# The order of the first weight rows and input tiles on two DMA queues, in a fused two-layer kernel

## The chip, the cores and the metric

One core of one Trainium2 chip. The metric is the device time of one execution in microseconds (us). Before the change it was 1615.32 us, the median of three executions (1615.10 to 1616.07).

## The reference

Two rounds of attention and feed-forward over 2048 tokens of width 1024, all in bf16. Attention is local and dilated: 32 heads, 8 keys each, 2 apart. Only the first step matters here: the normalization of the first 512 tokens and their product with the query weights.

```python
x = A_x                                              # (1, 2048, 1024)
x = x + _A_ref(_layernorm(x, axis=-1), A_wqkv, A_wo) # qkv = x @ wqkv, first of all
x = x + _B_ref(_layernorm(x, axis=-1), B_w1, B_w3, B_w2)
x = x + _A_ref(_layernorm(x, axis=-1), A_wqkv, A_wo)
x = x + _B_ref(_layernorm(x, axis=-1), B_w1, B_w3, B_w2)
```

## The kernel before

The kernel lists operations with what they read and write, a list scheduler in Python puts them in order, and they are emitted in that order. Each engine runs its own list in order. The keys in `reads` and `writes` only order the list: a wait on the chip exists only where the framework sees that two instructions touch the same tile. Two DMA queues are used: SyncE's ("SP") and ScalarE's ("AQ").

At the start, the query weights come in as eight rows, row k being 128 input dimensions by 1024 outputs (256 KB). The 512 tokens come as tiles 0 to 3 (256 KB each, tile 0 in two halves). Tiles 0 and 1 are only centred (their average is subtracted), transposed by TensorE, and multiplied with the rows as these arrive. Tiles 2 and 3 are normalized on VectorE first, and their product with all eight rows (64 matmuls at L524) follows.

```python
for hh in range(2):
    dma(128, x_sb[0][:, hh * 512:(hh + 1) * 512], ..., 0, queue="AQ" if hh else "SP")
dma(256, x_sb[1][:], xin[:, 1, :], [], ..., 0, queue="AQ")
rows = q_weights(0, "k", load=False)
wslots[0] = rows[:2]
for kk in (0, 1, 3, 4):
    rows[2](kk)                       # 256 KB each, on SyncE's queue
rows[2](2, queue="AQ")
load_x(0, 3, 4)                       # tile 3, SyncE
rows[2](5)
rows[2](6, 2)                         # rows 6 and 7 in one DMA of 512 KB
...
act(0.75, ...)                                               # ScalarE: half of tile 0's sum
dma(256, x_sb[2][:], xin[:, 2, :], [("part", 1)], ..., 0, queue="AQ")   # tile 2
act(1.15, ... accum_out=mean[:, 1:2]), [...], [("xn", 3), ("mean", 1)], -9)   # tile 1's average
...
wslots[1] = q_weights(1, "s")         # K weights: two DMAs of 1 MB on SyncE, issued after the rows
...
for t0, t1_ in ((0, 2), (2, 4), (4, 5), (5, 6), (6, 7), (7, 8)):
    dma(256 * (t1_ - t0), wo[:, t0:t1_, :], ...)
```

TensorE's order is fixed: transposes of tile 0 (L428), rows 0 and 1 on tile 0 (L510), transposes of tile 1, row 2 on tile 0, rows 0 to 2 on tile 1, rows 3 to 6 on both, transposes of tiles 2 and 3, row 7, then L524, then the K product (L347).

One thing isn't in the kernel's text but in the built program: DMAs of both queues are given eight completion semaphores in turn. From the ninth DMA on, an issue first waits until the last user of its semaphore has landed.

Of the kernel before, what the change touches and what calls it, by code (L numbers as in the profile page):

```python
# [156 lines left out]
def kernel(  # L157
# [15 lines left out]
    KT = D // P  # L173
# [26 lines left out]
    def alloc(name, shape, dt=BF16):  # L200
        return sb.tile(shape, dt, name=name)
# [13 lines left out]
    wo = alloc("wo", [P, KT, D])  # L215
# [18 lines left out]
    mean = alloc("mean", [P, 2], FP32)  # L234
    rsx = alloc("rsx", [P, NB], FP32)
    oT = [alloc(f"oT{i}", [P, KT, TCH]) for i in range(2)]
# [8 lines left out]
    def t1(n):  # L245
        return 0.15 + n / 960.0

    def dve(dur, emit, reads, writes, cls=2, **kw):
        return pr.add("DVE", dur, emit, reads, writes, cls, **kw)
# [4 lines left out]
    def dma(kb, dst, src, reads, writes, cls=3, transpose=False, queue="SP"):  # L254
        def emit(op):
            if queue == "AQ":
                nc.scalar.dma_start(dst, src)
            elif transpose:
                nc.sync.dma_start_transpose(dst, src)
            else:  # L260
                nc.sync.dma_start(dst, src)  # L261
        return pr.add(queue, 0.45, emit, reads, writes, cls, size=kb * 1024)
# [34 lines left out]
    def load_x(c, j0=0, j1=TPC, after=()):  # L297
        for j in range(j0, j1):
            n = c * TPC + j
            dma(256, x_sb[n][:], xin[:, n, :], after, [("x", n, 0), ("x", n, 1)], 0 if c == 0 else 3)  # L300
# [41 lines left out]
    def mm8(a, pairs, first, last, reads, lane=0, ncol=512, takes=True):  # L342
        n = len(pairs)

        def emit(op):
            for i, (w, r) in enumerate(pairs):
                nc.tensor.matmul(bank[a.bank][:, 0:ncol], lhsT=w, rhs=r, start=first and i == 0,  # L347
                                 stop=last and i == n - 1)
        return pr.add("PE", n * (ncol / 2400.0 + 0.0025), emit, reads, [], takes=[a], lane=lane, lag=0.17)

    def evac(add, dur, emit, last_mm, reads, writes, a, cls=0, **kw):
        op = add(dur, emit, reads, writes, cls, gives=[a], **kw)
        op.deps.add(last_mm)
        return op
# [3 lines left out]
    def q_weights(which, split, load=True, after=()):  # L358
        ids = [take_slot(), take_slot()]
        if not load:  # L360
            def row(kk, n=1, after=(), **kw):
                i = ids[kk // 4]
                v = slot[i][:].rearrange("p (k c) -> p k c", k=4)
                dma(256 * n, v[:, kk % 4:kk % 4 + n, :], wqkv_v[:, kk:kk + n, which * D:(which + 1) * D], after,
                    [("w", i, kk % 4 + z) for z in range(n)], 0, **kw)
            return ids, split, row
        for h, i in enumerate(ids):
            if split != "c":
                v = slot[i][:].rearrange("p (k c) -> p k c", k=4)
                dma(1024, v, wqkv_v[:, 4 * h:4 * h + 4, which * D:(which + 1) * D], after,  # L370
                    [("w", i, k) for k in range(4)], 3)
            else:
                v = slot[i][:].rearrange("p (k c) -> p k c", k=KT)
                dma(1024, v, wqkv_v[:, :, which * D + h * 512:which * D + (h + 1) * 512], [],
                    [("w", i, k) for k in range(4)], 3)
        return ids, split
# [18 lines left out]
    def q_tile(l, c, which, ws, b, keep=None):  # L395
        for m0 in range(0, KT, 2):
            i = n_sgt[0] % 4
            n_sgt[0] += 1
            for m in (m0, m0 + 1):
                a = Acc()  # L400
                lk = [q_lhs(ws, kk, m) for kk in range(KT)]
                op = mm8(a, [(w, xnT[b][:, kk, :]) for kk, (w, _) in enumerate(lk)], True, True,
                         list({k for _, k in lk}) + [("xnT", b, j) for j in range(TPC)] +
                         [("xnT", b, j, h) for j in range(TPC) for h in range(2)])
                evac(act, 0.59, lambda _, a=a, i=i, m=m: nc.scalar.copy(sgt[i][:, m % 2, :], bank[a.bank][:]), op, [],  # L405
                     [("sgt", i, m % 2)], a)
                if keep:
                    evac(act, 0.4, lambda _, a=a, m=m: nc.scalar.copy(keep[1][:, m, HALO:], bank[a.bank][:, 0:TCH]),
                         op, [], [(keep[0], m)], a)
            dma(256, spill_view(l, which, m0, c, ws[1] == "s"), sgt[i][:], [("sgt", i, 0), ("sgt", i, 1)],  # L410
                [("d", l, which, c, m0)], 1)
# [8 lines left out]
    def transposed(src, keys, dst, dkeys):  # L420
        for h, add, fn, dur in ((0, dve, nc.vector.tensor_copy, 0.42), (1, act, nc.scalar.copy, 0.59)):
            a = Acc()
            k0 = 4 * h

            def tr(op, a=a, k0=k0):
                pt = bank[a.bank][:].bitcast(BF16)
                for k in range(4):
                    nc.tensor.transpose(pt[:, k * P:(k + 1) * P], src[:, (k0 + k) * P:(k0 + k + 1) * P], ident[:])  # L428
            tro = pr.add("PE", 0.25, tr, [keys[h], "ident"], [], takes=[a], lag=0.17, lane=2)

            def emit(op, a=a, k0=k0, fn=fn):
                pt = bank[a.bank][:].bitcast(BF16)
                fn(dst[:, k0:k0 + 4, :], pt[:, 0:4 * P].rearrange("p (k t) -> p k t", k=4))
            evac(add, dur, emit, tro, [], dkeys[k0:k0 + 4], a, cls=-9)

    def q_first():
        for hh in range(2):
            dma(128, x_sb[0][:, hh * 512:(hh + 1) * 512], xin[:, 0, hh * 512:(hh + 1) * 512], [], [("x", 0, hh)], 0,
                queue="AQ" if hh else "SP")
        dma(256, x_sb[1][:], xin[:, 1, :], [], [("x", 1, 0), ("x", 1, 1)], 0, queue="AQ")  # L440
        rows = q_weights(0, "k", load=False)
        wslots[0] = rows[:2]
        for kk in (0, 1, 3, 4):
            rows[2](kk)
        rows[2](2, queue="AQ")
        load_x(0, 3, 4)
        rows[2](5)
        rows[2](6, 2)
        b, q, stats, root, apply = ln(0, first=True)
        ce = hT[:, 8:16, :]  # L450
        dve(0.45, lambda _: nc.vector.tensor_scalar(xn[2][:, 0:512], x_sb[0][:, 0:512], 0.0, 0.0, op0=ALU.add,
# [7 lines left out]
        act(1.15, lambda _: nc.scalar.activation(xn[3][:], x_sb[1][:], ACTF.Copy, scale=1.0 / D,  # L459
                                                 accum_out=mean[:, 1:2]), [("x", 1, 0), ("x", 1, 1)],  # L460
            [("xn", 3), ("mean", 1)], -9)
        for j in range(2):
            for h0, h1 in ((0, 1), (1, 2)) if j == 0 else ((0, 2),):
                dve(0.5 if j else 0.32, lambda _, j=j, c0=512 * h0, c1=512 * h1: nc.vector.tensor_scalar(
                    xn[j][:, c0:c1], x_sb[j][:, c0:c1], mean[:, j:j + 1], None, op0=ALU.subtract),
                    [("x", j, 0), ("x", j, 1), ("mean", j)], [("xn", j)] + [("xn", j, h) for h in range(h0, h1)], -9)
            transposed(xn[j], [("xn", j, h) for h in range(2)], ce[:, :, j * P:(j + 1) * P],
                       [("ce", j, k) for k in range(KT)])
# [72 lines left out]
        for which, key, tile_ in ((1, "kT", kT), (2, "vT", vT)):  # L541
            dve(0.11, lambda _, tile_=tile_: nc.vector.memset(tile_[:, :, 0:HALO], 0.0), [], [(key, "h")], 1)
            q_tile(0, 0, which, wslots[which], b, (key, tile_))
        for t0, t1_ in ((0, 2), (2, 4), (4, 5), (5, 6), (6, 7), (7, 8)):
            dma(256 * (t1_ - t0), wo[:, t0:t1_, :], wo_v[:, t0:t1_, :], [("d", 0, 2, 0, 6)], [("wo", t0)], 3)
        stage_no[0] += 1

# [24 lines left out]
    def t_stage(l, half):  # L572
# [46 lines left out]
        oh = half % 2  # L619
# [7 lines left out]
        for j in range(TCH // P):  # L627
            n = tok0 // P + j
            for hh in range(2):
                a = Acc()  # L630
                op = mm8(a, [(oT[oh][:, t, j * P:(j + 1) * P], wo[:, t, hh * 512:(hh + 1) * 512]) for t in range(KT)],
                         True, True, [("oT", oh, t) for t in range(KT)] + [("wo", t) for t in (0, 2, 4, 5, 6, 7)], lane=1)
                xs = x_sb[n][:, hh * 512:(hh + 1) * 512]
                evac(dve, t1(512), lambda _, xs=xs, a=a: nc.vector.tensor_tensor(xs, xs, bank[a.bank][:], op=ALU.add),  # L634
                     op, [("x", n, hh)], [("x", n, hh)], a)
# [72 lines left out]
    def attend(l, c):  # L708
        for r in range(R):
            t_stage(l, c * R + r)  # L710

    q_first()
    attend(0, 0)
    for c in range(1, NCH):
# [47 lines left out]
```

## Time and profile before

| | before |
|---|---|
| median of three executions | 1615.32 us |
| span of the profiled execution (which took 1616.3 us) | 1614.5 us |
| TensorE busy | 1609.9 us |
| TensorE's waits after the warm-up | 0.27 us for row 1, 0.79 us for rows 6-7 |

In the views, PE is TensorE and PEld its weight loads, DVE is VectorE, ACT is ScalarE; SPq and ACTq are the issue of a DMA on SyncE's and ScalarE's queue. `slot` is a weight buffer, `x` an input tile, `xn` a centred or normalized tile, `hT` and `xnT` transposed ones, `bank` an accumulator; L510 is a line of the kernel, and L285 the warm-up, ten matmuls on constants that use no loaded data. A line of three dots marks lines left out.

The first and third lines of the page, of the kernel before; busy time, share of the span and number of instructions of each engine:

```profile
span 1614.5 us, 19227 instructions
...
PE 1609.9 (100%) x7610; PEld 763.0 (47%) x7610; DVE 1121.6 (69%) x1904; ACT 330.8 (20%) x527; POOL 5.3 (0%) x28
```

TensorE's waits over the whole span, before (engine and line, what it waited for, us in total, times, the longest):

```profile
PE bank L510 <- DMA slot<-in_A_wqkv_dram: 1.1, 2, 0.8
PE bank L285 <- PEq L746: 0.8, 1, 0.8
```

The chain of waits in the first 24 us, before (start, us, what):

```profile
1.19 0.42 SPq L261
...
1.66 5.32 DMA slot<-in_A_wqkv_dram
6.98 0.02 issue
7.00 0.33 SPq L261
7.32 0.04 issue
7.37 5.98 DMA slot<-in_A_wqkv_dram
13.35 0.05 issue
13.40 1.05 PE bank L510 x8
...
16.21 6.99 PE bank L524 x64
```

This chain is the whole argument for the change: row 1 is loaded (to 6.98), its landing lets row 5 be issued (7.00), rows 6-7 are issued right behind it (7.37) and land at 13.35, and TensorE goes on at 13.40. TensorE's own timeline, before (start, us, engine, line, operation, tiles, form, count, idle time just before and what ended it):

```profile
5.02 1.00 PE L428 MATMUL bank<-ident,xn 128*128 128x128 bf16 x8
6.15 0.61 PE L510 MATMUL bank<-hT,slot 128*128 128x128 bf16 x8
7.03 0.62 PE L510 MATMUL bank<-hT,slot 128*128 128x128 bf16 x8 [0.27 <-DMA slot<-in_A_wqkv_dram]
7.57 0.62 PE L428 MATMUL bank<-ident,xn 128*128 128x128 bf16 x8
8.03 4.58 PE L510 MATMUL bank<-hT,slot 128*128 128x128 bf16 x56
13.40 1.05 PE L510 MATMUL bank<-hT,slot 128*128 128x256 bf16 x8 [0.79 <-DMA slot<-in_A_wqkv_dram]
14.28 1.06 PE L428 MATMUL bank<-ident,xn 128*128 128x128 bf16 x16
15.18 1.04 PE L510 MATMUL bank<-hT,slot 128*128 128x256 bf16 x8
16.05 7.15 PE L524 MATMUL bank<-xnT,slot 128*128 128x256 bf16 x64
```

From L524's start on TensorE never waits again. In every trace of this study the last weight load of the program comes 1595.6 to 1595.7 us after the first one of L524, except where the clock fell or the matmuls were ordered otherwise. So the start of L524 is the number to read: what it gains or loses, the span gains or loses.

ScalarE's list, before (ACTq is the issue of a DMA on its queue):

```profile
3.61 0.63 ACT L454 ACTIVATE xn<-x 128x512 bf16<-128x512 bf16 x1 [1.38 <-DMA x<-in_A_x_dram]
...
5.40 0.34 ACTq L257 DMA_DIRECT2D x<-in_A_x_dram  x1
5.85 1.06 ACT L459 ACTIVATE xn<-x 128x1024 bf16<-128x1024 bf16 x1 [1.52 <-DMA x<-in_A_x_dram]
```

The line at 5.40 is the issue of tile 2. It was meant to go out once the first average is on its way, but it waited until 5.38, when row 0 landed and its semaphore came free.

### The profile page before, as it was taken

Reading aid. Unit: us, or ns where it says so; the run is one execution under the profiler, and the core shown is the slowest. Engines: PE = TensorE matmul, PEld = TensorE weight load, DVE = VectorE, ACT = ScalarE, POOL = GpSimd, SP = SyncE. Lnnn points to the kernel's source line nnn. Section 1 sums busy time; section 2 is a strip of 40 time slices with the busy share of each in tenths; the row PEclk is TensorE's granted clock in tenths of the full one; section 3 lists DMA queues with packets and bytes.
Section 4 is the critical chain, followed back from the end, with each engine's and each line's share of the span. In section 5 each row is a group of like instructions: output and inputs, shape, how many; then the busy total and the mean of one; then the engine's idle time right before and its main releaser. Section 6 shows DMA issues by size and latency. Waiting matters only on the chain.

```text
span 1614.5 us, 19227 instructions
## 1 busy us (share of the span) xinstructions
PE 1609.9 (100%) x7610; PEld 763.0 (47%) x7610; DVE 1121.6 (69%) x1904; ACT 330.8 (20%) x527; POOL 5.3 (0%) x28
## 2 busy tenths in 40 slices
PE   9999999999999999999999999999999999999999
PEld 6555544444444444444444444444444444444444
DVE  5898888889889888888898729884298832211211
ACT  5423322021211222113211032110321101101110
POOL 1000000000000000000000000000000000000000
DMA  9834755395548664858545487355873564454451
GB/s 312 232 104 147 228 170 167 118 227 170 171 134 248 193 197 128 218 166 248 174 140 158 162 243 227 126 170 177 254 223 119 155 184 156 144 172 154 156 164 45
DMA packets 350777, 285.80 MB, mean 177 GB/s; under 512 B 72288, under 2 KB 344928, under 8 KB 350688
## 3 DMA queue, kind: packets, MB, share of 16 engines
q1 hardware_dynamic: 350112, 283.67, 58.4%
q8 instruction: 59, 0.97, 0.2%
q10 hardware_dynamic: 576, 0.92, 0.2%
q14 instruction: 30, 0.25, 0.0%
HBM read 238.94 MB, written 29.36 MB: 166 GB/s over the span
## 4 chain that ended last, share of the span: by engine, by line
PE 99%; DMA 1%; SPq 0%; issue 0%; DVE 0%
PE bank L347 98%; DMA slot<-in_A_wqkv_dram 1%; PE bank L524 0%; PE bank L510 0%; SPq L261 0%; PE bank L428 0%; DVE x L689 0%
## 5 line engine op out<-in xcount | busy, mean ns | idle before, releaser
L347 PE MATMUL bank<-xnT,slot 128*128 128x512 bf16 x5056 | 1094.2, 379 | 0.0
L347 PEld LDWEIGHTS <-slot 128*128 128x128 bf16 x5056 | 518.2, 102 | 572.9
L347 PE MATMUL bank<-slot,hT 128*128 128x512 bf16 (+2 forms) x1848 | 389.2, 373 | 0.0
L659 DVE TENSOR_TENSOR hT<-sg,bank 128x512 bf16<-128x512 bf16 x224 | 153.5, 685 | 212.5 <-PE bank L347 203.2
L265 DVE TENSOR_TENSOR scr<-scr 128x1024 bf16<-128x1024 bf16 (+3 forms) x576 | 292.8, 537 | 2.1
L347 PEld LDWEIGHTS <-hT 128*128 128x128 bf16 x1848 | 178.5, 98 | 208.7
L657 ACT ACTIVATE sg<-bank 128x512 bf16<-128x512 f32 x224 | 133.7, 597 | 654.1 <-PE bank L347 633.9
L265 DVE TENSOR_TENSOR scr<-qT,kT 128x2048 bf16<-128x2048 bf16 x128 | 153.9, 1218 | 73.1 <-DMA kT<-qkv_d 71.5
L405 ACT CAST sgt<-bank 128x512 bf16<-128x512 f32 x184 | 107.7, 586 | 288.9 <-PE bank L347 280.6
L265 DVE TENSOR_TENSOR scr<-pA,vT 128x2048 bf16<-128x2048 bf16 x128 | 152.7, 1219 | 0.4
L689 DVE TENSOR_TENSOR x<-x,bank 128x512 bf16<-128x512 bf16 (+1 forms) x66 | 43.7, 670 | 122.6 <-PE bank L347 122.4
L347 PE MATMUL bank<-wo,oT 128*128 128x512 bf16 x512 | 113.1, 379 | 0.0
L313 DVE BATCH_NORM_STATS2 st<-x 128x6 f32<-128x512 bf16 x124 | 81.5, 680 | 12.2 <-DMA x<-in_A_x_dram 11.8
L347 PEld LDWEIGHTS <-oT 128*128 128x128 bf16 x512 | 50.1, 98 | 60.4
L634 DVE TENSOR_TENSOR x<-x,bank 128x512 bf16<-128x512 bf16 x64 | 43.9, 685 | 35.6 <-PE bank L347 34.5
L320 ACT ACTIVATE sd<-mv,epst 128x4 f32<-128x4 f32 (+1 forms) x17 | 5.1, 298 | 183.7 <-DVE mv L316 183.4
L594 DVE STREAM_TRANSPOSE pB<-pA 128x2048 bf16<-128x2048 bf16 x16 | 37.0, 2310 | 0.4
L617 DVE STREAM_TRANSPOSE pA<-pB 128x2048 bf16<-128x2048 bf16 x16 | 37.0, 2310 | 0.4
L657 ACT ACT_TABLE_LOAD x20 | 25.7, 1283 | 51.0 <-PE bank L347 50.8
L265 DVE TENSOR_TENSOR pA<-scr 128x256 bf16<-128x256 bf16 x128 | 35.5, 284 | 0.3
L265 DVE TENSOR_TENSOR oT<-scr 128x256 bf16<-128x256 bf16 x128 | 33.8, 285 | 0.1
L327 DVE TENSOR_SCALAR xn<-x,mv,rstd 128x1024 bf16<-128x1024 bf16 x62 | 30.8, 541 | 3.7 <-DMA xnT<-xn 3.6
(60 smaller groups left out, 211.5 us busy)
## 6 DMA issues: line engine op xcount, KB each, us to landing
slot<-in_B_w_dram SPq DMA_DIRECT2D x160, 1024.0 KB, 6.0
slot<-in_A_wqkv_dram SPq DMA_DIRECT2D x28, 1024.0 KB, 5.2
qkv_d<-sgt SPq DMA_DIRECT2D x92, 256.0 KB, 3.6
qT<-qkv_d SPq DMA_DIRECT2D x16, 512.0 KB, 5.0
slot<-in_B_w_dram SPq DMA_DIRECT2D x16, 512.0 KB, 5.6
kT<-qkv_d SPq DMA_DIRECT2D x14, 544.0 KB, 6.7
vT<-qkv_d SPq DMA_DIRECT2D x14, 544.0 KB, 5.7
out_dram<-x SPq DMA_DIRECT2D x31, 128.0 KB, 4.4
```

What stands on the lines that cost most here:

```text
L265: return lambda _: nc.vector.tensor_tensor(o, a, b, op=op)
L313: dve(0.67, lambda _, hh=hh: nc.vector.bn_stats(st[q][:, j, hh, :], x_sb[n][:, hh * 512:(hh + 1) * 512]), [("x", n, hh)] + list(after), [( ...
L320: act(0.3, lambda _: nc.scalar.activation(sd[q][:, j0:j1], mv[q][:, j0:j1, 1], ACTF.Sqrt, bias=epst[:]), [("mv", q, j) for j in range(j0, ...
L327: dve(0.5, lambda _: nc.vector.tensor_scalar(xn[j][:], x_sb[n][:], mv[q][:, j, 0:1], rstd[q][:, j:j + 1], op0=ALU.subtract, op1=ALU.mult), ...
L347: nc.tensor.matmul(bank[a.bank][:, 0:ncol], lhsT=w, rhs=r, start=first and i == 0, stop=last and i == n - 1)
L405: evac(act, 0.59, lambda _, a=a, i=i, m=m: nc.scalar.copy(sgt[i][:, m % 2, :], bank[a.bank][:]), op, [], [("sgt", i, m % 2)], a)
L594: dve(2.31, lambda _: nc.vector.transpose(psmT[:].rearrange("p c d -> p (c d)"), psm[:].rearrange("p w s -> p (w s)")), allA, ["pB"])
L617: dve(2.31, lambda _: nc.vector.transpose(At[:].rearrange("p w s -> p (w s)"), AeT[:].rearrange("p c d -> p (c d)")), ["pB"], allA)
L634: evac(dve, t1(512), lambda _, xs=xs, a=a: nc.vector.tensor_tensor(xs, xs, bank[a.bank][:], op=ALU.add), op, [("x", n, hh)], [("x", n, hh) ...
L657: evac(act, 0.6, lambda _, i=i, a=ag: nc.scalar.activation(sg[i][:], bank[a.bank][:], ACTF.Silu), og, [], [("sg", i)], ag, table="silu")
L659: evac(dve, t1(512), lambda _, i=i, a=au, f=f: nc.vector.tensor_tensor(hT[:, f, :], sg[i][:], bank[a.bank][:], op=ALU.mult), ou, [("sg", i ...
L689: evac(dve, t1(cn), lambda _, xs=xs, a=a, cn=cn: nc.vector.tensor_tensor(xs, xs, bank[a.bank][:, 0:cn], op=ALU.add), op, [("x", n, hh)], [ ...
```

## The change

The intent: give rows 0 to 5 and 7 to SyncE's queue in the order in which TensorE wants them, let ScalarE's queue carry the tiles 1 and 2 and, early, row 6, and so have the last rows sooner. One load of wo is merged so that the number of DMAs stays the same.

```diff
-        for kk in (0, 1, 3, 4):
+        for kk in range(5):
             rows[2](kk)
-        rows[2](2, queue="AQ")
         load_x(0, 3, 4)
         rows[2](5)
-        rows[2](6, 2)
+        rows[2](7)
 ...
             [("xn", 3), ("mean", 1)], -9)
+        rows[2](6, queue="AQ", after=[("mean", 1)])
 ...
-        for t0, t1_ in ((0, 2), (2, 4), (4, 5), (5, 6), (6, 7), (7, 8)):
+        for t0, t1_ in ((0, 2), (2, 4), (4, 6), (6, 7), (7, 8)):
```

(The list of wo keys that the matmuls read is adapted likewise.)

More of the change, by code (lines that the diff above doesn't have):

```diff
@@ L631, in t_stage @@
                 op = mm8(a, [(oT[oh][:, t, j * P:(j + 1) * P], wo[:, t, hh * 512:(hh + 1) * 512]) for t in range(KT)],
-                         True, True, [("oT", oh, t) for t in range(KT)] + [("wo", t) for t in (0, 2, 4, 5, 6, 7)], lane=1)
+                         True, True, [("oT", oh, t) for t in range(KT)] + [("wo", t) for t in (0, 2, 4, 6, 7)], lane=1)
                 xs = x_sb[n][:, hh * 512:(hh + 1) * 512]
```

## The prediction

> **What bounds the kernel now.** The page has TensorE busy 1609.9 of 1614.5 us. In the waits, TensorE waits after its warm-up in two places only: 0.27 us at 7.03 for weight row 1, and 0.79 us at 13.40 for rows 6-7. After 13.40 it is dense to the end; the chain gives 98% to L347. So the change acts only on the first 14 us, and what it wins there should reach the end.
>
> **Why rows 6-7 come late.** By the trace's semaphore operands, DMAs of both queues take eight completion semaphores in turn, and an issue waits until the semaphore's last user has landed. Row 5's issue (7.00) followed row 1's landing (6.98); rows 6-7 (512 KB) went behind it, at 7.37, and landed at 13.35. Thirteen of sixteen parts were there by 11.98, the last three only at 13.25 to 13.35. Tile 2's issue on ScalarE (5.40) likewise followed row 0's landing (5.38), not its average (4.33).
>
> **What changes.**
> - Row 2 leaves ScalarE's queue. The queues share bandwidth evenly: from 4 to 5 us the trace has 182 KB on SyncE's, 186 KB on ScalarE's. The Trainium skill ("DMA: Bandwidth & Descriptors", "Issuing engines are not separate DMA queues") says that both run on the same 16 DMA engines and interleave; the trace agrees. Row 1 then no longer competes with row 2: about 200 KB less ahead of it, at 370 KB/us, lets it land near 6.4 (estimate), and row 5 is issued then, row 7 right after.
> - Row 6 goes out from ScalarE at about 7.0 (tile 1's average ends at 6.99). Tile 2 took 4.26 us from issue to landing there, so row 6 lands near 11.4, row 7 near 11.5 (both 10.7 to 12.8).
> - ScalarE pays one issue, 0.45 us, ahead of the copy at 6.90 (tile 0, upper half), first needed by row 4's matmuls near 10.8: off the path.
> - wo in five DMAs, not six: off the path.
>
> **Critical path after.** TensorE is dense from 8.03 to 12.6 (rows 2 to 5). Row 6's matmuls (0.87) then start without the 0.79 us wait. The next limit is close: VectorE's normalization starts at tile 2's landing (9.66) and has tile 3 ready at 13.74. Row 6 ends at 13.45, tile 2's transposes at 13.95, tile 3's at 14.4, row 7 at 15.3, where L524's 64 matmuls start (before: 16.05). So more than 0.8 us isn't to be had unless tile 1's average comes earlier. Later, x transposes and K weights land at 21.2 and 19.4, needed at about 22.2.
>
> **Time.** 1615.3 - 0.8 = 1614.5 us; range 1613.8 to 1615.5. Faster by over 2%: 0.005; within 2%: 0.99; slower: 0.005.
>
> **What would show it.** (1) Row 5 issued before 6.7. (2) No wait of TensorE for a slot near 12.6, or under 0.3 us. (3) L524 starting at 15.1 to 15.5. (4) Row 6 issued at 7.0 to 7.5, row 7 landed before 13.
>
> **What would make it wrong.** (a) The order of the semaphores turns: tile 2 might take the one of tile 0's first half and be issued near 4.3 (tile 1's average then starts 0.2 us earlier: gain about 1.0), or row 6 might wait on ScalarE for row 2's or 3's landing, land after 12.6, and give back part. (b) The straggling tail hits row 6. (c) Tile 2, sharing with row 5, lands after 9.9 and VectorE becomes the limit. (d) Run-to-run scatter (1615.1 to 1616.07) is as large as the effect.

## The result, and the profile after

The kernel after took 1615.03 us, the median of six executions (1614.75 to 1615.25); before, in the same rounds, 1615.43 (six executions, 1614.88 to 1616.07). The ratio is 0.9997, 95% interval 0.9984 to 1.001: the same. Ratios here are the mean time of one kernel's fast runs over that of the other's of the same rounds, so not quite the ratio of the medians.

The profile after, first and third lines of the page:

```profile
span 1613.4 us, 19079 instructions
...
PE 1601.8 (99%) x7463; PEld 763.1 (47%) x7610; DVE 1121.7 (70%) x1904; ACT 330.7 (20%) x527; POOL 5.3 (0%) x28
```

TensorE's lower busy time is no saving: 147 matmul records of 7610 are missing from this trace, while all 7610 weight loads are there. TensorE's waits, after:

```profile
PE bank L285 <- PEq L746: 0.8, 1, 0.8
PE bank L428 <- DVE xn L464: 0.2, 1, 0.2
PE bank L510 <- DVE hT L433: 0.2, 1, 0.2
```

No wait for a weight row is left. TensorE's timeline, after:

```profile
5.40 0.94 PE L428 MATMUL bank<-ident,xn 128*128 128x128 bf16 x8 [0.20 <-DVE xn L464]
6.52 1.05 PE L510 MATMUL bank<-hT,slot 128*128 128x128 bf16 x16 [0.18 <-DVE hT L433]
7.41 0.61 PE L428 MATMUL bank<-ident,xn 128*128 128x128 bf16 x8
7.86 5.45 PE L510 MATMUL bank<-hT,slot 128*128 128x128 bf16 x64
13.14 1.06 PE L428 MATMUL bank<-ident,xn 128*128 128x128 bf16 x16
14.04 1.04 PE L510 MATMUL bank<-hT,slot 128*128 128x256 bf16 x8
14.91 7.15 PE L524 MATMUL bank<-xnT,slot 128*128 128x256 bf16 x64
```

L524 starts at 14.91, 1.14 us earlier than in the profile before, and the span is 1.1 us shorter. But the median of the times moved by 0.40 us only. ScalarE's list, after:

```profile
3.98 0.63 ACT L453 ACTIVATE xn<-x 128x512 bf16<-128x512 bf16 x1 [1.76 <-DMA x<-in_A_x_dram]
3.99 0.33 ACTq L257 DMA_DIRECT2D x<-in_A_x_dram  x1
...
5.38 1.06 ACT L458 ACTIVATE xn<-x 128x1024 bf16<-128x1024 bf16 x1 [0.67 <-DMA x<-in_A_x_dram]
5.42 0.33 ACTq L257 DMA_DIRECT2D slot<-in_A_wqkv_dram  x1
...
6.43 0.56 ACT L433 COPY hT<-bank 128x512 bf16<-128x512 bf16 x1
```

Two things differ from what I expected. Tile 2 is issued at 3.99: one more DMA now stands on SyncE ahead of tile 3, so that in the turn of the semaphores tile 2 comes before tile 3 and takes the one of tile 0's first half, which had landed at 3.73. And both tile 2 and row 6 are issued as the activation in front of them begins (0.01 and 0.04 us after its start), not as it ends: the DMA reads nothing that the activation writes, so no wait is emitted, and ScalarE issues it while the activation runs. The copy that I had expected to pay for the issue starts at 6.43, 0.09 us after the start of the accumulator read before it, as in the kernel before (6.90 after 6.81).

That left one question: why 1.1 us in the two profiles and 0.4 us in the times? The profiled execution of before took 1616.3 us, longer than each of its six timed ones.

### The profile page after: what moved, and what is told of

Its sections match the earlier page's. It is cut to its first block, busy times and chain, and to the rows that moved or that the text cites. A ratio compares the mean times of both kernels' runs of the same rounds, so it can differ in the third digit from the quotient of the medians.

```text
span 1613.4 us, 19079 instructions
## 1 busy us (share of the span) xinstructions
PE 1601.8 (99%) x7463; PEld 763.1 (47%) x7610; DVE 1121.7 (70%) x1904; ACT 330.7 (20%) x527; POOL 5.3 (0%) x28
## 4 chain that ended last, share of the span: by engine, by line
PE 99%; issue 1%; DMA 0%; DVE 0%; ACT 0%
PE bank L347 98%; PE bank L510 0%; PE bank L524 0%; DMA x<-in_A_x_dram 0%; PE bank L428 0%; ACT xn L453 0%; DVE hT L433 0%; DVE xn L464 0%; DVE x L689 0%; DVE mean L456 0%; ACT L281 0%
## 5 line engine op out<-in xcount | busy, mean ns | idle before, releaser
L313 DVE BATCH_NORM_STATS2 st<-x 128x6 f32<-128x512 bf16 x124 | 81.5, 680 | 12.0 <-DMA x<-in_A_x_dram 11.5
```

The costliest lines, as they stand in the source:

```text
L313: dve(0.67, lambda _, hh=hh: nc.vector.bn_stats(st[q][:, j, hh, :], x_sb[n][:, hh * 512:(hh + 1) * 512]), [("x", n, hh)] + list(after), [( ...
```

## The experiments

Twelve runs were made. Those of one set ran on the same chip, and the three sets ran on three different chips. The names of the theories in the quoted expectations:
- T1: TensorE's wait for rows 6-7 binds in every execution before, and the change removes it. T1': for that row 6 needs a DMA of its own.
- T2: the gain comes from row 2's move.
- T3: the first profile caught a rare straggling tail.
- P and U: the scatter of the times before comes from the tail of rows 6-7 (P), or from upstream, from row 1's landing (U).
- Q and R: row 6 is late on ScalarE's queue because of large loads issued ahead of it on the other queue (Q), or for another reason (R).
- V and W: tile 2's landing is the next limit (V), or row 1's landing alone matters (W).

### Set 1: both kernels again, and each half of the change alone

**before_again**: no edit.

> The kernel before, unchanged, for a second trace and more times. Theory T1 (rows 6-7 bind TensorE in every run): rows 6-7 land at 13.0 to 13.6 again, TensorE waits 0.6 to 1.0 us for them, L524 starts near 16.0. Rival T3 (the first profile, whose execution took 1616.3 us, more than each of the six timed ones, caught a rare straggling tail of three DMA engines): they land near 12.2, TensorE waits under 0.3 us, L524 starts near 15.3 to 15.6, and that is why the times differ by 0.4 us only, not by the 1.1 us of the two spans. Ratio of times 1.000 by construction.

Measured: 1615.39 us, median of five (1614.83 to 1616.12); before itself, in nine executions, 1615.48 (1614.95 to 1616.35). Rows 6-7 landed at 11.09, L524 started at 14.57, span 1613.0. TensorE's waits:

```profile
PE bank L285 <- PEq L746: 0.8, 1, 0.8
PE bank L510 <- DVE hT L433: 0.3, 1, 0.3
```

and the last line of its timeline up to L524:

```profile
14.57 7.15 PE L524 MATMUL bank<-xnT,slot 128*128 128x256 bf16 x64
```

The same program has no wait for a weight row at all here, and its span is shorter than that of the kernel after. So T1 is wrong as a statement about every execution. T3 is right in that the wait belonged to the first trace alone, but its numbers missed on the early side (rows 6-7 near 12.2, L524 at 15.3 to 15.6 expected), and "rare" is too strong if it is meant of slow executions: 19 of the 38 times of before (its runs in all sets, and before_again's five) are above 1615.40, which none of the 16 of after is.

**after_again**: no edit.

> The kernel after, unchanged, for a second trace and more times. T1: no wait for rows 6 or 7 again, L524 starts at 14.6 to 15.1 (it moves with the landing of tile 0, 3.96 in the first trace against 3.58 before), time 0.4 to 0.9 us under before. T3: time 0.2 to 0.5 us under before.

Measured: 1614.93 us (1614.88 to 1615.17). No wait for a row, L524 at 14.94, span 1613.4. The median is 0.55 us under before, which lies in T1's range (0.4 to 0.9) and just outside T3's (0.2 to 0.5); what rules T1 out is the trace of before_again. In this trace too tile 0 landed late (4.09).

**row2_only**:

```diff
-        for kk in (0, 1, 3, 4):
+        for kk in range(5):
             rows[2](kk)
-        rows[2](2, queue="AQ")
```

> Only row 2 moves to SyncE's queue; rows 6-7 stay one DMA of 512 KB behind row 5 on SyncE. By the program's semaphores tile 2 then takes the semaphore of tile 0's first half, as in the kernel after. T2 (the gain comes from row 2's move: row 1 lands earlier, so row 5 and all behind it are issued earlier, and tile 2 and tile 1's average come earlier): row 5 issued near 6.1, rows 6-7 near 6.5, landing near 12.4, TensorE's wait for them under 0.3 us, L524 at 14.9 to 15.2, time as after. T1' (row 6 must have a DMA of its own): rows 6-7 land after 13.0, wait over 0.5 us, L524 at 15.6 or later.

Measured: 1615.09 us (1614.86 to 1615.17). Tile 2 issued at 3.69, row 5 at 5.71, rows 6-7 landed at 11.49 in one DMA, no wait of TensorE for them, L524 at 14.59 (L523 in this kernel), all earlier than T2 had it:

```profile
14.59 7.15 PE L523 MATMUL bank<-xnT,slot 128*128 128x256 bf16 x64
```

T1' falls: rows 6-7 land in time in one DMA. That this half of the change gives what the whole gives, as T2 says, is read from the times (none of the five above 1615.17, and six of before's nine in the same rounds above 1615.40); the trace alone can't show it, since before_again on the same chip starts L524 just as early.

**row6_only**:

```diff
-        rows[2](6, 2)
+        rows[2](7)
 ...
+        rows[2](6, queue="AQ", after=[("mean", 1)])
```

(and the merged load of wo)

> Only row 6 moves, in a DMA of its own, to ScalarE's queue; row 2 stays there too. By the program's semaphores tile 2 still waits for row 0, and row 6 waits on ScalarE for row 3's landing (7.66 before). T1: row 6 issued near 7.7, lands at 11.5 to 12.3, no wait near 12.6 over 0.2 us, tile 1's average still starts near 5.85, L524 at 15.2 to 15.4, time 0.5 to 0.8 us under before if before waits as in its first profile. T2: L524 near 16.0 as before. ScalarE, held by the wait until 7.7, copies tile 0's upper half about 1.2 us later (near 8.1); if that half were needed before row 4's matmuls near 10.8, TensorE would show a wait for it.

Measured: 1616.99 us (1615.77 to 1620.08); the median is 1.51 us above that of before in the same rounds (ratio 1.0013, interval 1.0000 to 1.0025). My expectation was wrong here, T1's and T2's alike. Row 6 was issued at 7.51 as foreseen, but landed at 12.95 (first of its sixteen parts) to 15.49 (last). This trace is of the slowest of the five executions (1620.08); three of the others took 1615.77 to 1616.99, so its wait too is the size of one execution. TensorE's wait, in its timeline:

```profile
15.53 1.05 PE L511 MATMUL bank<-hT,slot 128*128 128x256 bf16 x8 [3.24 <-DMA slot<-in_A_wqkv_dram]
```

And the wait cost more than itself. The stretches after it, for this kernel (from and to in us, the length, busy time of PE, PEld, DVE, ACT and POOL with the number of instructions, then the granted TensorE clock, the DMA engines' busy share and GB/s):

```profile
15.50:16.40 0.90, 0.87 (x8) 0.79 (x9) 0.00 (x0) 0.00 (x0) 0.73 (x4) 1.00 2.35 323
16.40:18.00 1.60, 1.60 (x20) 1.52 (x19) 0.88 (x3) 0.62 (x2) 0.73 (x4) 0.64 0.73 92
18.00:20.00 2.00, 2.00 (x11) 1.45 (x10) 0.42 (x1) 2.00 (x5) 0.00 (x0) 0.50 0.38 79
```

Soon after an idle time of 3.24 us the clock is granted at 0.64 and then 0.50 of full speed. The Trainium skill ("TensorE: Matmul & The Clock Gate", Part 1) says that the clock falls to half after about one idle window of 3.4 us; the trace agrees in size only, since the idle time was 3.24 us, a little under that, and the fall came 1.3 us after the work resumed (from 16.9 to 20.3 us the step from one matmul to the next is doubled). The record has a mean clock of 0.999 for this execution and the one at 1619.33, and 1.000 for the other three. From row 6's start to L524's, this trace needs 3.9 us (15.53 to 19.43); the first trace of before needs 2.65 (13.40 to 16.05).

What held row 6 up? Two K-weight DMAs of 1 MB had been issued on SyncE at 6.90 and 7.38, just ahead of it. That is theory Q, looked at in set 2.

### Set 2: what scatters, and what held row 6

**split_only**:

```diff
-        rows[2](6, 2)
+        rows[2](6)
+        rows[2](7)
```

(and the merged load of wo; both rows stay on SyncE, row 2 stays on ScalarE)

> Before, with rows 6 and 7 as two DMAs of 256 KB, both still on SyncE behind row 5; row 2 stays on ScalarE's queue, tile 2 still waits for row 0. Theory P (the scatter of the times before, 1614.8 to 1616.4, is the last parts of the 512 KB pair landing after TensorE needs row 6, near 12.4): row 6 lands some 0.7 us ahead of the pair, TensorE's wait is gone in nearly all executions, times narrow to 1614.7 to 1615.3 as after. Rival U (the scatter comes from upstream: row 1's landing, which gates row 5 and all behind it, 6.0 in one trace and 7.0 in the other): times still reach 1615.6 to 1616.3 in two or more of five.

Measured: 1615.42 us (1614.83 to 1616.60); before in the same rounds 1615.64 (1614.96 to 1617.11). Two of five times are above 1615.6, as U said; P falls as the only source of the scatter. It isn't empty: in the first trace of before 13 of the 16 parts of rows 6-7 were there by 11.98, before TensorE had run out of work near 12.6, and the last three, at 13.25 to 13.35, made the wait of 0.79 us. The trace of split_only, of an execution of 1615.81 us, shows where it comes from: row 1's last parts landed at 7.18 and 7.46 while the other fourteen were there by 5.90.

```profile
PE bank L511 <- DMA slot<-in_A_wqkv_dram: 0.9, 1, 0.9
```

TensorE waits 0.89 us for row 1 (its matmuls start at 7.51) and for no other row: row 6 landed at 11.73, in time. L524 starts at 15.58, 1.01 us later than in before_again (which ran on another chip).

**row6_k_held**:

```diff
+        rows[2](6, queue="AQ", after=[("ce", 1, KT - 1)])
+        for i in (2, 3):
+            act(0.2, lambda _, i=i: nc.scalar.copy(slot[i][:, 0:1], epst[:]),
+                [("ce", 1, KT - 1), "eps"], [("w", i, 0)], -9)
```

(in place of row6_only's line; the copies write a column of each K-weight slot, so that the loads must wait for them; the loads overwrite it)

> row6_only, but row 6 is issued on ScalarE still later (behind tile 1's upper copy, near 8.0; it was 7.5 there), and the two K-weight DMAs of 1 MB each (6.9 and 7.4 there) are held on SyncE by two tiny ScalarE copies into their slots until row 6 is out (near 8.4). Theory Q (row 6 came late in row6_only, 12.9 to 15.5, because 2 MB of K weights were issued ahead of it, though on the other queue): row 6 lands by 11.5, TensorE's wait is under 0.3 us, times near 1615.0 to 1615.4, none over 1616. Rival R (ScalarE's queue is slow for an issue this late, or the two queues share evenly and row 6 was late for another reason): row 6 lands after 12.5 and TensorE waits 0.5 us or more.

Measured: 1616.38 us (1616.15 to 1617.14). Row 6 was issued at 8.39 and landed at 10.97 (first part) to 12.92 (last); TensorE waited 0.21 us for it. Neither expectation met its numbers: it did not land by 11.5 (Q), and it did land after 12.5 as R had it, but TensorE did not wait 0.5 us or more for it (R). But from issue to the first part it took 2.58 us, and 5.44 us in row6_only; to the last part 4.53 us, and 7.98. So with the K weights ahead of it, on the other queue, row 6 took some 3 us longer, which supports Q but doesn't prove it: row 6 was also issued 0.88 us later, and two single executions are compared, one of them the slowest of its five; what remains late in this trace goes with row 1, whose last part landed at 7.23 and held rows 5 and 7 back on SyncE. The times say nothing about Q: the new operations also changed TensorE's order (tile 3's transposes came behind row 7), and L524 started at 16.07.

**row2_split**: row2_only and split_only together, so rows 0 to 7 all on SyncE in eight DMAs, and tiles only on ScalarE.

> Candidate: all of rows 0 to 7 on SyncE (0-4, tile 3, 5, 6, 7, each 256 KB), ScalarE's queue carries tiles only. Rows 6 and 7 by 11.5, no wait of TensorE, L524 at 14.5 to 14.9 (depends on tile 0's landing), times 1614.7 to 1615.2: level with after. If moving row 6 to ScalarE is worth anything, after is faster by 0.1 us or more.

Measured: 1614.84 us (1614.78 to 1615.22). Rows 6 and 7 at 11.07 and 12.01, no wait for a row, L524 at 14.54, span 1613.2.

**before_3**: no edit, one execution.

> The kernel before once more, for a third trace. If the wait for rows 6-7 alone makes its scatter, its span is 1613.0 plus TensorE's wait for them plus the delay of tile 0's landing against 3.5 us, within 0.2 us.

Measured: 1615.34 us, span 1613.5. Row 1 landed at 6.70, rows 6-7 at 11.75, TensorE's waits list none for a weight row; L524 started at 15.07. The expectation misses: without a wait for rows 6-7 it gives a span near 1613.1. The excess of 0.5 us over before_again goes with row 1 and with tile 2, which landed at 9.61 (9.07 there), so that VectorE had tile 3 ready only at 13.69, after TensorE had come to the transposes (13.09).

### Set 3: tile 2 apart from row 1, and the two best side by side

**row2_tile2_late**: row2_only with one emitted instruction moved.

```diff
+        placed = pr.place()
+        late = next(o for o in placed if ("x", 2, 0) in o.writes)
+        placed.remove(late)
+        placed.insert(1 + next(i for i, o in enumerate(placed) if ("mean", 1) in o.writes), late)
-        for op in pr.place():
+        for op in placed:
```

> row2_only with one instruction moved: tile 2's issue comes behind tile 1's average on ScalarE, not ahead of it; TensorE's and VectorE's order is unchanged. By the program's semaphores tile 2 then waits for row 1 (near 6.2), and row 5 for row 0 (near 4.9), so the rows come early and tile 2 late. Theory V (tile 2's landing is the next limit, through VectorE's normalization: 4.05 us from its landing to tile 3 ready): tile 2 lands at 9.9 to 10.4, tile 3 is ready at 14.0 to 14.4, L524 starts near 15.4, times 1615.5 to 1615.9, narrow, 0.5 to 0.8 us over row2_only. Rival W (row 1's landing alone makes the gain of row 2's move): L524 at 14.6 to 14.9 and times 1614.9 to 1615.2 as row2_only.

Measured: 1619.23 us (1617.98 to 1619.89), ratio to before in the same rounds 1.0025 (1.0011 to 1.0039). W's numbers fail, V is right in kind and much too small. Row 1 landed early (5.76), rows 6-7 at 12.31, and still TensorE's largest wait is this:

```profile
PE bank L428 <- DVE xn L327: 2.2, 1, 2.2
```

Tile 2 was issued at 5.78, 0.04 us after the first K-weight DMA of 1 MB on SyncE, and landed at 12.09, 6.31 us after its issue, not at 9.9 to 10.4. VectorE had tile 3 ready 4.07 us later (16.16; its normalization started at 12.11), as the 4.05 us read from the first profile say, and L524 started at 17.55. This is Q once more, with another load: a 256 KB DMA issued on ScalarE's queue behind large ones on SyncE's lands late. Because tile 2 came so much later than intended, the run does not tell what it was built for: how much of row 2's gain comes through row 1 and how much through the earlier tile 2. The trace is of the fastest of the five executions; I have none of those at 1619 and more, but the record gives their mean clock as 0.999, and 1.000 for the two at 1618, so the clock probably fell in them as in row6_only.

**after_3**, **row2_split_2**, **before_4**: no edits to after, row2_split and before; before_4 is one execution.

> The kernel after again, on the same chip as row2_split_2: times 1614.75 to 1615.25, median near 1614.95; row 1 lands under 6.4, no wait for rows 6 or 7.

> The candidate again, on the same chip as after: if moving row 6 to ScalarE is worth nothing, the medians differ by under 0.15 us; if the candidate is better for lack of it, it is 0.1 to 0.3 us faster.

> The kernel before, a fourth trace. Theory U: its span over 1613.0 follows row 1's landing: about 1613.0 for 6.0, 1613.5 for 6.7, 1614.5 for 7.0, within 0.4 us.

Measured: after_3 1615.07 us (1614.84 to 1615.40), row2_split_2 1614.97 (1614.80 to 1615.54), before in the same rounds 1615.04 (1614.84 to 1615.60), before_4 1615.03 with row 1 at 6.16 and span 1613.2, as U expected. after_3's times reach above the expected 1615.25; the rest came as expected (row 1 at 6.11, no wait). On this chip, in these rounds, before is as fast as both: nothing scattered far. The two best differ by 0.10 us, less than their ranges, so moving row 6 to ScalarE is worth nothing that these runs can show. No version beats before by more than its scatter.

### The traces side by side

Landing times are the last of a DMA's sixteen completion counts in the trace, in us:

```
trace            row 2 on   tile 0   row 1   row 6 (6-7)   tile 2   L524 starts   span
before           ScalarE     3.58     6.98      13.35        9.66      16.05      1614.5
before_again     ScalarE     3.52     6.01      11.09        9.07      14.57      1613.0
before_3         ScalarE     3.64     6.70      11.75        9.61      15.07      1613.5
before_4         ScalarE     3.63     6.16      11.32        9.29      14.75      1613.2
split_only       ScalarE     3.45     7.46      11.73       10.11      15.58      1614.0
row6_only        ScalarE     3.62     6.04      15.49        9.32      19.43      1618.3
row6_k_held      ScalarE     3.58     7.23      12.92        9.87      16.07      1614.7
after            SyncE       3.96     6.11      10.98        9.13      14.91      1613.4
after_again      SyncE       4.09     6.14      11.04        9.34      14.94      1613.4
after_3          SyncE       4.08     6.11      10.88        9.22      15.00      1613.5
row2_only        SyncE       3.66     5.70      11.49        8.81      14.59      1613.3
row2_split       SyncE       3.55     6.31      11.07        9.08      14.54      1613.2
row2_split_2     SyncE       3.61     5.85      10.60        8.57      14.50      1613.1
row2_tile2_late  SyncE       3.54     5.76      12.31       12.09      17.55      1616.2
```

Row 1, with row 2 beside it on ScalarE's queue, lands at 6.65 on average and at 7.46 at worst (seven traces); with row 2 behind it on SyncE's, at 6.00 and at worst 6.31 (seven traces). A late row 1 costs three times: TensorE wants it near 6.5; by the semaphores row 5 is issued only after it, and rows 6-7 behind row 5; and in the traces of before tile 2 is late together with it.

The chips differ, though. Set 2's chip has the landings at 6.70, 7.23 and 7.46, and row2_split's 6.31; on the chips of sets 1 and 3 the two groups hardly differ (6.01, 6.04 and 6.16 against 5.70 to 6.14). The times carry more: of the kernels with row 2 on SyncE and tile 2 early (after, row2_only, row2_split) 1 of 31 times is above 1615.40, and 19 of 38 of before. That moving row 2 narrows the scatter is shown by this; that it does so through row 1, and not through the earlier tile 2, is argued.

The landings also show in what order loads are served. In all 14 traces, the 13 to 15 loads issued in the first 8.5 us landed in the order of their issue, over both queues together, but for three pairs, in each of which a 256 KB load on ScalarE's queue overtook a larger one issued 0.04 to 0.52 us before it on SyncE's.

## Why the prediction was right or wrong

The predicted range (1613.8 to 1615.5, around 1614.5) holds the measured 1615.03, and "within 2%" was never in doubt. But the range also holds the time of before in the same rounds (1615.43), so lying inside it says little. The points:

1. **"TensorE waits ... 0.79 us at 13.40 for rows 6-7", taken as what before does.** This is the step that was mis-sized. One of four traces of before has that wait; the other three have none. The gain is the removal of a scatter, not of a constant: measured as medians of the same rounds it was 0.40 us in the first comparison, 0.55 in set 1 (1615.48 to 1614.93) and -0.03 in set 3 (1615.04 to 1615.07). The lowest times hardly differ: 1614.83 before, 1614.75 after. The sign was in sight: the profiled execution had taken longer than each timed one. The prediction named the scatter as its risk (d), but its size was taken from the one trace.
2. **Row 1 lands earlier, and row 5 is issued then.** Right: 6.11, and row 5 at 6.13 (predicted: before 6.7). That it matters was shown in split_only (a wait of 0.89 us for row 1 and for no other row); the times of row2_only, between 1614.86 and 1615.17, fit it.
3. **Row 6 issued at 7.0, landing near 11.4.** The landing was right in size (10.98) by luck: the issue came 1.6 us earlier (5.42), and the way from there took 5.56 us, not 4.26. The issue did not wait for the end of the activation listed before it (6.44). Had the issue come where I expected it, row 6 would have been at risk: in row6_only, issued at 7.51 behind 2 MB of K weights, it landed at 15.49. In the prediction I took 4.26 us from issue to landing as a property of the queue; the runs show 4.53 to 7.98 for row 6 on that queue; what had been issued before it is the likely reason (Q).
4. **"ScalarE pays one issue, 0.45 us".** Wrong, and harmless: it paid nothing that the trace shows.
5. **Risk (a), tile 2 taking tile 0's semaphore.** It came true: issued at 3.99. The prediction put its effect at 0.2 us through tile 1's average, which did start earlier (5.38, not 5.85). That tile 2's landing itself binds when it is late enough was shown by row2_tile2_late (12.09).
6. **L524 at 15.1 to 15.5.** It was 14.91, which is risk (a)'s case, in spite of tile 0 landing 0.4 us later than in the first trace of before. The prediction's next limit, tile 3 ready at 13.74, kept tile 2's landing at 9.66; it came at 9.13, and tile 3 was ready at 13.21.
7. **No wait for a slot near 12.6; row 7 landed before 13; dense after L524.** Right in all three traces of after (row 7 at 11.82, 12.06 and 12.11).

Two things stay open. Tile 0 landed at 3.96 to 4.09 in the three traces of after and at 3.45 to 3.66 in the eleven others, although the kernel after issues the same DMAs up to that time as row2_split does; I have no cause. And in row2_only and row2_split the end of the program, from the last weight load on, takes 3.09 to 3.12 us and in before and after 2.90 to 2.92, so that the 0.4 us by which row2_split is ahead of after at L524 shrink to 0.2 us at the end; one late piece is SyncE's last DRAIN, an instruction of the program's end (0.14 us, against 0.01). The cause of the late parts of row 1 in some executions isn't known either: in these traces they go with row 2 on the other queue, and, where the chip is known, with set 2's chip; split_only shows that they cost the time, not why two parts of sixteen come 1.3 us after the rest.

## What to carry to other kernels

Before you price a wait read from one profile, compare that execution's time with the timed ones: if it is the slowest of them, the wait may be its own, and a second trace of the same kernel is the cheapest experiment there is. Here a second queue added no bandwidth while the DMA engines were busy (377 GB/s on two queues from 4 to 5 us in before, 408 on SyncE's alone from 11 to 12 us in after): what counted was what had been issued before, on both queues, so issue small urgent loads ahead of the large ones and put a load that is needed first alone in front rather than beside its successor. Where completion semaphores are used in turn, adding or moving one DMA changes which issue waits for which landing; list these pairs anew after every such change.

## What the Trainium skill lacked or had wrong

- "DMA: Bandwidth & Descriptors", "Issuing engines are not separate DMA queues": it says that DMAs of all issuing engines run on the same 16 DMA engines and interleave. The runs agree in the bandwidth (182 and 186 KB on the two queues from 4 to 5 us, before). What it lacks is that a small DMA can be held up by large ones of the other queue issued shortly before: 256 KB took 7.98 us to land with 2 MB issued ahead on the other queue (row6_only), and 4.53 us without (row6_k_held).
- The same page, "Queues, rings and completion order": each engine goes round between the queues that have work, packet by packet. In row6_only row 6's first packets moved at 11.11, 3.60 us after its issue, while SyncE's queue moved data throughout; so the turn is not enough to foretell a landing. How the descriptors of two queues get into the rings is not said, and the runs don't show it.
- The same page, "Latency and other measured facts", names two DMA engines as usually slower and guesses that the cause lies with DMAs issued by GpSimd. Loads from SyncE's queue also have late parts: in split_only 14 of row 1's 16 parts were there by 5.90, and the last two at 7.18 and 7.46. The trace doesn't tell which engines.
- No page says of a DMA's issue on ScalarE that it goes out while the activation listed before it runs: 5.42 against 5.38 to 6.44, in the kernel after.
- No page speaks of completion semaphores used in turn, where an issue waits for an earlier landing (a property of the built program): row 5 waited until row 1 had landed (6.98), and was issued at 7.00, in the kernel before.
